# RWKV attention and a squared-ReLU feed-forward in one kernel: a new issue order of all steps, with two quarters of W2 loaded first

## The chip, the cores and the metric

One core of one Trainium2 chip. The metric is device time in microseconds for one launch; lower is better.

## The reference

Per batch and head a 48x48 state decays by `w` each step, takes in the outer product of k and v, and is read with r; `u` weighs the present step. The result, 3072 tokens of 384 numbers, goes through a feed-forward with a squared ReLU:

```python
batch, n_heads, seq, head_dim = (4, 8, 768, 48)      # r, k, v; w, u: n_heads x head_dim
for t in range(S):
    cur = np.einsum('bhd,bhe->bhde', u[None] * kt, vt)
    y[:, :, t] = np.einsum('bhd,bhde->bhe', rt, state + cur)
    state = w[None, :, :, None] * state + np.einsum('bhd,bhe->bhde', kt, vt)
...
n_tokens, d_model, d_ff = (3072, 384, 2048)
h = np.maximum(x @ w_in, 0.0)
return (h * h @ w_out).astype(np.float32)
```

## The kernel before

The tokens are cut into 24 tiles of 128 (tile i is chunk i // 4 of batch i % 4, so the state of a tile comes from tile i - 4). Every piece of work is a *step* with a short name, and one long string, `ORDER`, lists all steps. A step reads `name.arguments:engine/buffers`: `kh.4:G/5` is step kh of tile 4 on GpSimd with buffer 5. The engine letters are P (TensorE, PE in the profile), D (VectorE, DVE), A (ScalarE, ACT), G (GpSimd, POOL) and S (SyncE, SP, which only issues transfers). The string is walked once and each step is put on its engine's queue; an engine runs its queue strictly in the order of the string, and semaphores between engines see to it that data are there and buffers free. There is no other scheduler. `POOLS` says how many buffers each kind has (7 for loads of r, k and v, 2 PSUM banks for F1, 2 for F2, 4 for the rest of PE's work).

The steps of an attention tile, with the lines of the kernel before:

- `ld.r`, `ld.k`, `ld.v` (L320): load 128 tokens, 192 KB each, in rows of 192 bytes.
- `kh`, `rh` (L336, L339): k and r times powers of w, to `rk`. `T` and `Tc` (L363, L260) transpose `rk` on PE and copy it to `rkT`; `XB` (L369) does both as one DMA transpose issued by SP.
- `A` (L376) multiplies them, `Bm` (L384) masks the product. `P0`, `P1`, `du`, `dv` (L342, L346, L349, L354) make the part with u. `vb` (L260, L262) turns v to bf16.
- `Y` (L392, L394) is the tile's output, `xs` (L411) adds dv to it; `U` (L403), `ts` (L421), `S0` and `S` (L418, L424) carry the state on.
- `X` and `xTc` (L429, L260) transpose the output on PE and copy it to `xT`; `xX` (L436) does both as a DMA transpose issued by SP.

The feed-forward works on groups of tiles: tiles 0 and 1 alone (groups 0 and 1), then eleven groups of two. `F1.g.s` (L445) makes 512 numbers per row of the hidden layer of group g: s is a slice of 256 columns of `w_in` for a pair, and two such slices for a single tile. `re` (L453, L455) is the ReLU out of PSUM, which frees the F1 bank, and `sq` (L460, L462, L464) squares it. `F2.i.q` (L472) adds quarter q of the hidden layer to the output of tile i: four matmuls of 384 columns with `W2[q]`. After the four quarters `os` (L260, L262) copies the bank and `out` (L487) stores it.

The weights come in float32. `lW.0.s` (L324, by SP) loads slice s of `w_in` to one of four staging buffers and `cW.0.s` (L260, L262) casts it. `W.0.2` and `W.1.q` (L333, by POOL) are transfers that cast on the way: slice 2 of `w_in` and the four quarters of `w_out`. So W2 comes through POOL's DMA queue, and all else through SP's (or, for the stores marked A, ACT's). `w`, `u`, `wc`, `shw`, `shu`, `logw`, `Wk`, `Wt` and their like prepare the powers of w once. `Z.n.b` (L481) is n matmuls on the identity whose result nobody reads.

Early in the order stand the loads of tiles 0 to 3 and the slices of `w_in`, then the first F1 (`F1.1.0`), and only then `W.1.0`, `W.0.2`, `W.1.1`, `W.1.2`, `W.1.3`.

Of the kernel before, what the change touches and what calls it, by code (L numbers as in the profile page):

```python
# [20 lines left out]
ld.r.1:S/0 w:A ld.k.1:S/0 u:S Z.48.5:P tab:A ld.k.0:S/1 ld.k.2:S/2 shw:D ld.r.0:S/1 logw:A ld.r.2:S/2 Wt:A/0 P0.1:D/0  # L21
Wk:A/1 lW.0.6:S/0 kh.1:D/0 ld.v.1:S/0 rh.1:D shu:D ld.k.3:S/3 T.1:P/0 kh.0:D/1 Z.16.5:P P1.1:G Tc.1:A/0 kh.2:D/2
rh.0:D ld.v.3:S/1 WtS:A rh.2:D P0.2:G/1 A.1:P/1/2 WkS:A T.0:P/3 lW.0.1:S/1 Z.16.5:P P1.2:D ld.r.3:S/3 Tc.0:A/1
du.1:D/0 P0.0:D/2 cW.0.6:A ld.v.0:S/2 A.0:P/0/3 dv.1:G Bm.1.1:D/0 Z.6.5:P du.2:D/1 T.2:P/2 P1.0:G Bm.1.0:D/1
ld.v.2:S/3 Z.22.5:P Tc.2:A/2 Bm.0.0:D/2 Bm.0.1:D/3 lW.0.0:S/2 vb.1:A/0 lW.0.5:S/3 kh.3:D/3 Y.1:P/1 cW.0.1:A lW.0.7:S/0
A.2:P/0/2 xs.1:D/0 Z.4.5:P P0.3:G/3 vb.3:A/1 du.0:D/2 lW.0.4:S/1 X.1:P/3 Z.8.5:P rh.3:D wc:S xTc.1:A/0 Bm.2.0:D/4
vb.0:A/2 T.3:P/1 ld.k.4:S/4 dv.0:D Y.0:P/3 Z.13.5:P Tc.3:A/3 vb.2:G/3 Bm.2.1:D/5 P1.3:G xs.0:D/1 A.3:P/0/2 X.0:P/1
cW.0.0:A U.0:P/3 dv.2:G Bm.3.0:D/1 Z.6.7:P xTc.0:A/1 du.3:D/3 lW.0.3:S/2 F1.1.0:P/0 Bm.3.1:D/0 ld.r.4:S/4 F1.0.0:P/1
re.1.0:D/0 cW.0.7:G Y.2:P/0 Y.3:P/1 re.0.0:A/1 ld.k.5:S/5 xs.2:D/2 cW.0.5:A W.1.0:G dv.3:D F1.1.3:P/0 cW.0.4:A W.0.2:G
X.2:P/2 F1.0.3:P/1 re.1.3:D/2 ld.r.5:S/5 xTc.2:A/0 W.1.1:G U.2:P/0 xs.3:D/3 F1.0.2:P/0 re.0.3:A/3 sq.1.3:D2/0 WLcol:A  # L30
X.3:P/2 F1.1.2:P/1 re.0.2:D/4 xTc.3:A WLm:G U.3:P/1 F1.2.1:P/0 re.1.2:A/5 W.1.2:G sq.0.3:A0/1 F1.2.5:P/1 re.2.1:D/2
W.1.3:G sq.0.0:A0/2 U.1:P/2 S0.2:D re.2.5:A/3 F1.2.4:P/0 sq.0.2:D2/3 cW.0.3:A S0.0:D F1.2.7:P/1 re.2.4:D/1 sq.1.0:A0/4
# [36 lines left out]
S.11:D re.6.5:A/0 ts.13:D/0 F2.9.2:P os.8:A/2 out.7:S P0.18:D/0 sq.6.0:A0/5 Y.13:P/2 ts.12:D/1 ld.k.21:S/3
sq.6.6:A0/13 F2.9.3:P P1.18:G xs.13:D/3 sq.6.5:A0/15 ld.v.16:S/1 F2.10.0:P/1 Bm.14.1:D/2 dv.14:G X.13:P/0 du.15:D/0  # L70
F2.10.1:P ld.r.20:S/4 P0.16:G/4 re.6.7:D/2 xTc.13:A Y.14:P/1 vb.15:A/6 F1.7.5:P/0 kh.20:G/6 xs.14:D/4 ld.k.22:S/6
os.9:A/0 F1.7.6:P/1 S.12:D A.16:P/2/3 xX.14:S/0 re.7.6:A/1 P1.17:G A.17:P/0/1 F2.11.0:P/0 sq.6.7:A0/16 Bm.17.1:D/1
sq.6.4:A0/17 S.13:G F1.7.1:P/1 ld.v.20:S/6 Bm.16.1:D/0 re.7.5:A/4 F2.11.1:P ld.k.19:S/5 Bm.17.0:D/2 dv.15:G Y.15:P/1
re.7.1:D/3 ld.r.19:S/6 F1.7.0:P/0 xs.15:D/0 rh.20:G F1.7.3:P/1 re.7.0:A/0 ld.r.23:S/5 P1.16:D U.15:P/3 sq.7.1:A0/20
F2.10.2:P du.16:D/1 re.7.3:A/2 U.14:P/0 xX.15:S F1.7.2:P/0 P0.20:D/1 vb.16:A/3 dv.16:G Bm.16.0:D/3 sq.7.3:A0/18
F1.7.4:P/1 out.5:S re.7.2:A/5 rh.18:D F2.11.2:P vb.18:A/1 out.8:S sq.7.6:D2/21 re.7.4:A/3 F2.10.3:P sq.7.5:D2/19
ld.r.21:S/2 kh.19:D/5 vb.17:A/2 F1.7.7:P/0 ld.k.23:S/1 sq.7.4:A0/22 rh.19:D Y.16:P/1 kh.22:D/4 re.7.7:A/2 Y.17:P/2
XB.19:S/4 xs.16:D/2 sq.7.2:A0/23 F2.11.3:P kh.21:D/2 os.10:A/3 F1.8.2:P/1 du.17:D/2 sq.7.0:A0/26 XB.18:S/6 ts.14:D/1
F1.8.0:P/0 dv.17:G re.8.2:A/1 F2.12.0:P/1 os.11:A/2 re.8.0:D/4 vb.20:G/0 sq.8.2:A0/25 F1.8.3:P/1 xX.16:S/1 S.14:G
# [30 lines left out]
    A=["bA{0}0", "bA{0}1"],  # L110
    ld=["{0}{1}"],
# [7 lines left out]
def kernel(  # L119
# [417 lines left out]
```

## Time and profile before

| | |
|---|---|
| median of 3 runs | 176.94 us (176.59 to 178.07) |
| span of the profiled execution | 175.6 us |
| PE busy | 165.1 us (94%), 1813 matmuls |
| DVE / ACT / POOL busy | 140.6 / 109.4 / 69.2 us |
| read from and written to HBM | 20.46 and 4.72 MB |
| r, k, v loads | 72 of 192 KB, 3.8 to 4.1 us from issue to landing (medians) |
| W2 quarters (POOL's queue) | 4 of 384 KB as written, 10.2 us |
| transposes by DMA | 14 of rk (4.2 us), 10 of x (2.9 us) |
| granted PE clock | full in all slices |

The page gives no separate time for the profiled execution: its span is 175.6 us, and the runs' median is 1.3 us over it. A busy PE isn't PE at its peak, since matmuls are pipelined and their ends are modelled. What matters more is when PE stands still, and what it waits for there.

### The profile page before, as it was taken

To read this page: it belongs to the slowest core of one execution; us is meant where nothing else is said; L and a number is where in the kernel's file an instruction comes from. 1 tells how busy PE (TensorE), PEld (TensorE's weight loads), DVE (VectorE), ACT (ScalarE), POOL (GpSimd) and SP (SyncE) were. 2 spreads that over 40 slices of the span, in tenths; PEclk is the share of its full clock that TensorE was granted. 3 is DMA by queue.
4 is the path that set the end of the run, shared out by engine and by line. 5 is a ranking of instruction groups with operands and counts; after the bars stand their busy time and mean duration, and the time that the engine had idled before them with its cause. 6 is when DMAs were issued, how large, how long until landed. Compare 5 with 4: busy or idle time off the path is not lost.

```text
span 175.6 us, 4601 instructions
## 1 busy us (share of the span) xinstructions
PE 165.1 (94%) x1813; PEld 127.0 (72%) x1813; DVE 140.6 (80%) x278; ACT 109.4 (62%) x203; POOL 69.2 (39%) x84
## 2 busy tenths in 40 slices
PE   4888797899999999999999999999999999999991
PEld 4767695666778778777767787777778677787760
DVE  4699877499899998999989899899988667853620
ACT  2479498249399987886668669669478132164401
POOL 4073582035358394926282960600960302000000
PEclk9999999999999999999999999999999999999999
DMA  5999999989899999999999979989971422110041
GB/s 105 218 217 236 315 231 187 192 166 220 163 210 106 246 207 134 232 159 242 170 162 214 212 142 223 155 203 191 199 157 26 157 90 62 33 45 0 4 169 55
DMA packets 102277, 28.36 MB, mean 161 GB/s; under 512 B 94824, under 2 KB 102256, under 8 KB 102256
## 3 DMA queue, kind: packets, MB, share of 16 engines
q1 hardware_dynamic: 100360, 26.10, 75.4%
q0 software_dynamic: 1744, 1.77, 6.1%
q8 instruction: 14, 0.23, 0.6%
q10 hardware_dynamic: 152, 0.20, 0.3%
q14 instruction: 7, 0.06, 0.1%
HBM read 20.46 MB, written 4.72 MB: 143 GB/s over the span
## 4 chain that ended last, share of the span: by engine, by line
PE 80%; DMA 10%; SPq 4%; POOL 1%; issue 1%; ACT 0%; POOLq 0%
PE bank L472 36%; PE bank L445 33%; DMA wsa<-in_moe_w_in_dram 6%; DMA W<-in_moe_w_in_dram 5%; SPq L320 4%; PE bank L376 3%; PE bank L394 2%; PE bank L392 2%; PE bank L403 2%; PE bank L363 2%; PE bank L429 1%; POOL W L262 0%; SPq L324 0%; POOL W L333 0%; ACT os L260 0%
## 5 line engine op out<-in xcount | busy, mean ns | idle before, releaser
L445 PE MATMUL bank<-xT,W 128*128 128x256 bf16 (+1 forms) x624 | 74.4, 264 | 1.6 <-ACT W L260 0.9
L472 PE MATMUL bank<-W,hq 128*128 128x384 bf16 x384 | 73.6, 326 | 1.0 <-DMA W<-in_moe_w_out_dram 1.0
L453 ACT ACTIVATE hr<-bank 128x512 bf16<-128x512 f32 x71 | 42.0, 597 | 38.9 <-PE bank L445 36.3
L445 PEld LDWEIGHTS <-W 128*128 128x128 bf16 x624 | 55.3, 98 | 12.3 <-ACT W L260 1.2
L472 PEld LDWEIGHTS <-hq 128*128 128x128 bf16 x384 | 35.6, 98 | 19.0 <-issue 1.2
L460 ACT ACTIVATE hq<-hr 128x512 bf16<-128x512 bf16 x57 | 34.7, 629 | 2.5 <-DVE hr L455 2.4
L384 DVE TENSOR_TENSOR Bm<-bank,maskJT 128x512 bf16<-128x512 f32 x48 | 31.4, 683 | 3.0 <-PE bank L376 3.0
L346 POOL TENSOR_TENSOR P<-P,ub 128x384 f32<-128x384 f32 x14 | 15.2, 1086 | 35.5 <-DVE P L342 29.8
L455 DVE TENSOR_SCALAR hr<-bank 128x512 bf16<-128x512 f32 x25 | 17.1, 689 | 11.9 <-PE bank L445 8.3
L354 POOL TENSOR_TENSOR dv<-ldv,du 128x384 f32<-128x384 f32 x19 | 16.6, 886 | 23.7 <-DVE du L349 21.6
L464 DVE TENSOR_TENSOR hq<-hr 128x512 bf16<-128x512 bf16 x35 | 15.0, 457 | 1.7 <-ACT hr L453 1.7
L411 DVE TENSOR_TENSOR xs<-bank,dv 128x384 bf16<-128x384 f32 x24 | 13.2, 553 | 2.8 <-PE bank L394 2.2
L260 ACT COPY os<-bank 128x384 f32<-128x384 f32 x18 | 8.6, 477 | 8.1 <-PE bank L472 8.1
L481 PE MATMUL bank<-identity 128*128 128x128 bf16 x139 | 11.0, 242 | 2.3 <-POOL identity masks.py:199 2.3
L349 DVE TENSOR_REDUCE du<-P 128x8 f32<-128x384 f32 x24 | 12.9, 544 | 0.2 <-POOL P L346 0.2
L342 POOL TENSOR_TENSOR P<-ldr,ldk 128x384 f32<-128x384 f32 x11 | 11.3, 1024 | 2.4 <-DMA ldr<-in_r_dram 2.4
L260 ACT COPY rkT<-bank 128x1024 bf16<-128x1024 bf16 x10 | 10.1, 1015 | 2.8 <-PE bank L363 2.7
L481 PEld LDWEIGHTS <-identity 128*128 128x128 bf16 x139 | 9.7, 111 | 2.5 <-POOL identity masks.py:199 2.3
L424 POOL TENSOR_TENSOR S0W<-ts,WLm 128x384 bf16<-128x384 f32 x7 | 7.4, 1060 | 10.0 <-PE bank L472 6.7
L394 PE MATMUL bank<-vb,Bm 128*128 128x48 bf16 x192 | 10.8, 183 | 0.4 <-ACT vb L260 0.3
L394 PEld LDWEIGHTS <-Bm 128*128 128x128 bf16 x192 | 9.5, 96 | 1.4 <-issue 0.6
L260 ACT CAST vb<-ldv 128x384 bf16<-128x384 f32 x19 | 9.6, 512 | 0.0
(61 smaller groups left out, 163.8 us busy)
## 6 DMA issues: line engine op xcount, KB each, us to landing
ldr<-in_r_dram SPq DMA_DIRECT2D x24, 192.0 KB, 4.0
ldk<-in_k_dram SPq DMA_DIRECT2D x24, 192.0 KB, 4.1
ldv<-in_v_dram SPq DMA_DIRECT2D x24, 192.0 KB, 3.8
out_dram<-os SPq DMA_DIRECT2D x23, 192.0 KB, 2.1
wsa<-in_moe_w_in_dram SPq DMA_DIRECT2D x7, 384.0 KB, 4.8
W<-in_moe_w_out_dram POOLq DMA_DIRECT2D x4, 384.0 KB, 10.2
rkT<-rk SPq DMA_TRANSPOSE x14, 4.2
W<-in_moe_w_in_dram POOLq DMA_DIRECT2D x1, 192.0 KB, 8.1
```

Source lines behind the costliest of these rows:

```text
L260: e.copy(o, a)
L346: e.tensor_mul(t, t, ub)
L354: e.tensor_mul(dvb[slot[f"dv{i}"]], loaded("v", i), t)
L384: e.tensor_mul(Bmb[slot[f"Bm{i}{h}"]], heads(bank(f"bA{i}{h}"), 128), mask_b)
L394: e.matmul(y[:, hc, D * h : D * (h + 1)], m[h][:, hc, :], vb[:, 2 * hc + h, :], start=(c == 0), stop=True, skip_group_check=True,)
L445: e.matmul(hp[:, fi, :], W1[f // 2][:, c, 128 * (f % 2) : 128 * (f % 2 + 1)], xt[:, c, :], start=(c == 0), stop=(c == CCH - 1), skip_group ...
L453: e.activation(hr, hp, AF.Relu)
L455: e.tensor_scalar_max(hr, hp, 0.0)
L460: e.activation(hq, hr, AF.Square)
L464: e.tensor_mul(hq, hr, hr)
L472: e.matmul(bank(f"bO{i}", "bO")[:, 0:d_model], hqb[slot[f"hq{g},{f // m}"]][:, at : at + L], W2[q][:, f % 4, :], start=(f == 0), stop=(f = ...
L481: e.matmul(banks[b][:, 0:128], identity, identity, start=True, stop=True, skip_group_check=True)
```

## The change

`ORDER` is written anew from its first step to its last: 952 steps in place of 961, with the same buffers (`POOLS`) and the same groups. What differs beside the order:

- F2 takes a tile's quarters in any order. A list per tile notes which have been issued, so that the first starts the sum in PSUM and the last ends it.
- `W.1.2` and `W.1.3` are the first things that POOL issues after its setup, and `W.1.0` follows `P1.0`. The first F1 is `F1.1.3`, which uses slices 6 and 7, so these two are loaded first; the first F2 uses quarter 3. `lW.0.4` and `lW.0.5` now come behind the loads of tiles 4 and 5.
- 11 stores are issued by ACT (before: 1) and 13 by SP (before: 23).
- 16 x tiles are transposed by DMA (before: 10), 8 by PE (before: 14); of their copies 4 go to ACT and 4 to DVE (before: 14 to ACT). `XB` stays at 14.
- Work goes from DVE and ACT to POOL: kh 16 steps there (before 5), P0 18 (11), P1 18 (14), S 10 (7), rh 8 (6), vb 7 (3), cW 3 (1); dv goes the other way, 10 (19). ACT has 62 of the squares (before 57) and 69 of the ReLUs (71).
- The warm-up matmuls Z number 151 (before 139), 80 of them in front of the first T.
- `rh` may come before `kh` of the same tile, so it names the buffer too.

The order's beginning and end, and the code:

```diff
 ORDER = """
-ld.r.1:S/0 w:A ld.k.1:S/0 u:S Z.48.5:P tab:A ld.k.0:S/1 ld.k.2:S/2 shw:D ld.r.0:S/1 logw:A ld.r.2:S/2 Wt:A/0 P0.1:D/0
-Wk:A/1 lW.0.6:S/0 kh.1:D/0 ld.v.1:S/0 rh.1:D shu:D ld.k.3:S/3 T.1:P/0 kh.0:D/1 Z.16.5:P P1.1:G Tc.1:A/0 kh.2:D/2
-rh.0:D ld.v.3:S/1 WtS:A rh.2:D P0.2:G/1 A.1:P/1/2 WkS:A T.0:P/3 lW.0.1:S/1 Z.16.5:P P1.2:D ld.r.3:S/3 Tc.0:A/1
-du.1:D/0 P0.0:D/2 cW.0.6:A ld.v.0:S/2 A.0:P/0/3 dv.1:G Bm.1.1:D/0 Z.6.5:P du.2:D/1 T.2:P/2 P1.0:G Bm.1.0:D/1
-ld.v.2:S/3 Z.22.5:P Tc.2:A/2 Bm.0.0:D/2 Bm.0.1:D/3 lW.0.0:S/2 vb.1:A/0 lW.0.5:S/3 kh.3:D/3 Y.1:P/1 cW.0.1:A lW.0.7:S/0
-A.2:P/0/2 xs.1:D/0 Z.4.5:P P0.3:G/3 vb.3:A/1 du.0:D/2 lW.0.4:S/1 X.1:P/3 Z.8.5:P rh.3:D wc:S xTc.1:A/0 Bm.2.0:D/4
-vb.0:A/2 T.3:P/1 ld.k.4:S/4 dv.0:D Y.0:P/3 Z.13.5:P Tc.3:A/3 vb.2:G/3 Bm.2.1:D/5 P1.3:G xs.0:D/1 A.3:P/0/2 X.0:P/1
-cW.0.0:A U.0:P/3 dv.2:G Bm.3.0:D/1 Z.6.7:P xTc.0:A/1 du.3:D/3 lW.0.3:S/2 F1.1.0:P/0 Bm.3.1:D/0 ld.r.4:S/4 F1.0.0:P/1
-re.1.0:D/0 cW.0.7:G Y.2:P/0 Y.3:P/1 re.0.0:A/1 ld.k.5:S/5 xs.2:D/2 cW.0.5:A W.1.0:G dv.3:D F1.1.3:P/0 cW.0.4:A W.0.2:G
-X.2:P/2 F1.0.3:P/1 re.1.3:D/2 ld.r.5:S/5 xTc.2:A/0 W.1.1:G U.2:P/0 xs.3:D/3 F1.0.2:P/0 re.0.3:A/3 sq.1.3:D2/0 WLcol:A
-X.3:P/2 F1.1.2:P/1 re.0.2:D/4 xTc.3:A WLm:G U.3:P/1 F1.2.1:P/0 re.1.2:A/5 W.1.2:G sq.0.3:A0/1 F1.2.5:P/1 re.2.1:D/2
...
-re.12.7:A/5 F2.21.2:P re.12.4:A/3 sq.12.7:D1/24 F2.21.3:P F1.12.0:P/0 os.21:D/0 F2.20.0:P/1 re.12.0:A/2 F1.12.2:P/1
-F2.20.1:P re.12.2:D/5 F1.12.3:P/0 sq.12.0:D2/25 sq.12.1:D2/8 F2.20.2:P sq.12.6:D2/4 re.12.3:A/2 sq.12.2:D2/3
-F2.23.0:P/0 sq.12.4:D2/28 sq.12.3:A0/7 F2.20.3:P sq.12.5:A0/0 F2.23.1:P os.20:D/2 F2.23.2:P out.20:S F2.23.3:P
-out.19:S F2.22.0:P/1 out.21:S os.23:D/1 F2.22.1:P out.23:S F2.22.2:P F2.22.3:P os.22:A/2 out.22:A
+ld.k.1:S/0 ld.r.0:S/0 ld.r.1:S/1 u:S w:A ld.k.0:S/1 ld.k.2:S/2 wc:S ld.r.2:S/2 ld.k.3:S/3 ld.r.3:S/3 ld.v.1:S/0 shw:D
+tab:A P0.1:D/0 shu:D logw:A Wk:A/0 lW.0.7:S/0 W.1.2:G Wt:A/1 WkS:A ld.v.0:S/1 kh.1:D/0 rh.1:D lW.0.6:S/1 W.1.3:G WtS:A
+P1.1:G kh.0:D/1 Z.80.5:P T.1:P/0 rh.0:D Tc.1:A/0 Z.18.5:P A.1:P/1/2 WLcol:A T.0:P/3 rh.2:D/2 kh.2:D Bm.1.0:D/0 du.1:D/0
+Tc.0:A/1 T.2:P/0 P0.0:G/1 Tc.2:A/2 lW.0.0:S/2 lW.0.1:S/3 vb.1:A/0 P1.0:G Bm.1.1:D/1 W.1.0:G P0.2:G/2 Z.9.5:P A.0:P/1/3
+rh.3:D/3 kh.3:D ld.v.3:S/2 cW.0.7:A Z.16.5:P T.3:P/2 WLm:G vb.0:A/1 lW.0.3:S/0 ld.v.2:S/3 du.0:D/1 Y.1:P/0 Bm.0.1:D/2
+dv.1:G ld.k.5:S/4 P0.3:G/3 Bm.0.0:D/3 ld.r.5:S/4 Tc.3:A/3 xs.1:D/0 Z.20.5:P X.1:P/3 ld.k.4:S/5 dv.0:G ld.r.4:S/5
+ld.v.5:S/4 P1.3:D cW.0.6:A Y.0:P/1 Z.8.5:P A.3:P/0/2 lW.0.4:S/1 xs.0:D/1 X.0:P/1 xTc.1:D/0 F1.1.3:P/0 xTc.0:A/1
+Bm.3.1:D/4 W.0.2:G P1.2:G A.2:P/3/1 W.1.1:G re.1.3:A/0 F1.0.3:P/1 Bm.3.0:D/5 du.3:D/2 cW.0.0:G lW.0.5:S/2 dv.3:G
+re.0.3:D/1 Bm.2.1:D/0 U.1:P/2 U.0:P/0 cW.0.1:A ld.r.7:S/6 sq.1.3:A0/0 du.2:D/3 sq.0.3:A0/1 vb.3:A/2 Bm.2.0:D/1 S0.0:D
+F1.1.0:P/0 cW.0.3:G dv.2:D F1.0.0:P/1 F2.1.3:P/1 re.1.0:A/2 re.0.0:A/3 ld.v.4:S/5 Y.3:P/1 ld.k.7:S/6 F2.0.3:P/0 vb.2:A/3
+F1.1.1:P/0 U.3:P/3 Y.2:P/0 xs.3:D/2 ld.r.6:S/1 sq.1.0:D2/2 F1.0.1:P/1 S0.3:D ld.k.9:S/0 ld.k.6:S/1 U.2:P/1 F2.1.0:P
+ld.v.6:S/6 re.1.1:A/4 ld.r.8:S/0 X.3:P/3 kh.5:G/4 ld.v.8:S/0 xs.2:D/3 rh.5:G kh.4:G/5 P0.5:D/4 sq.1.1:A0/3 re.0.1:A/5
+ld.k.10:S/2 P0.4:G/0 F2.1.1:P sq.0.0:A0/4 ld.k.8:S/3 xTc.3:A/0 vb.5:G/4 X.2:P/0 S0.2:D xTc.2:A F2.0.0:P T.5:P/1 cW.0.4:G
+rh.4:D P0.7:G/1 Tc.5:A/4 S0.1:D F1.2.2:P/0 ld.k.13:S/4 rh.6:G/6 kh.7:G/0 sq.0.1:D2/5 ld.r.9:S/2 T.4:P/3 F1.2.7:P/1
+Tc.4:A/5 P1.5:D ld.r.13:S/3 U.5:P/0 P1.4:D ts.5:D/0 re.2.7:D/0 ld.v.7:S/1 F2.0.1:P P0.6:G/3 re.2.2:A/1 kh.6:G P1.6:G
+A.5:P/2/1 Bm.5.1:D/2 A.4:P/3/0 F1.2.4:P/0 cW.0.5:A P1.7:G ld.r.10:S/4 ld.v.13:S/2 Bm.5.0:D/3 F1.1.2:P/1 kh.8:G/1
...
+sq.11.7:D2/25 F2.20.2:P/1 F1.12.6:P/1 sq.11.1:A0/26 out.18:A sq.11.0:A0/0 re.11.3:A/4 sq.12.0:D2/24 sq.11.3:D2/10
+out.17:S re.12.6:D/0 F2.20.3:P F2.21.0:P F2.21.3:P F1.12.4:P/0 F1.12.3:P/1 re.12.4:A/1 re.12.3:D/5 F2.21.1:P
+sq.12.3:D2/29 F1.12.2:P/0 out.16:A re.12.2:A/3 sq.12.2:D2/1 F2.20.1:P F1.12.7:P/1 re.12.7:D/2 F2.20.0:P sq.12.6:D2/28
+F1.12.1:P/0 os.20:A/1 sq.12.7:A0/5 out.20:S F1.12.5:P/1 re.12.1:D/4 re.12.5:A/5 os.21:A/0 sq.12.1:D2/27 sq.12.5:D2/2
+F2.23.3:P/1 F2.23.1:P sq.12.4:D2/12 out.21:S F2.22.3:P/0 F2.23.0:P F2.22.1:P F2.23.2:P F2.22.2:P os.23:D/2 out.19:S
+F2.22.0:P os.22:A/1 out.23:S out.22:A
 """
...
-    lW=["ws{0}{1}"], kh=["rk{0}"], P0=["P{0}"], du=["dv{0}"], vb=["vb{0}"], T=["bT{0}"], Tc=["rkT{0}"], XB=["rkT{0}"],
+    lW=["ws{0}{1}"], kh=["rk{0}"], rh=["rk{0}"], P0=["P{0}"], du=["dv{0}"], vb=["vb{0}"], T=["bT{0}"], Tc=["rkT{0}"], XB=["rkT{0}"],
...
+    quarters = {}
...
         def F2(e, i, q):
             g, j = group_of[i]
             n = len(GROUP[g])
             m = 4 // n
+            done = quarters.setdefault(i, [])
+            done.append(q)
             for f in range(4 * q, 4 * q + 4):
                 at = L * n * (f % m) + L * j
                 e.matmul(
                     bank(f"bO{i}", "bO")[:, 0:d_model],
                     hqb[slot[f"hq{g},{f // m}"]][:, at : at + L],
                     W2[q][:, f % 4, :],
-                    start=(f == 0), stop=(f == FCH - 1), skip_group_check=True,
+                    start=(f == 4 * q and len(done) == 1), stop=(f == 4 * q + 3 and len(done) == 4),
+                    skip_group_check=True,
                 )
```

## The prediction, made before the changed kernel was run

> **What bounds the kernel now.** I read the slices first, then busy time by stretch, then PE's waits, then the DMA queues. Two rows of the slices, PE and the DMA engines:
>
> ```profile
> PE   4888797899999999999999999999999999999991
> ...
> DMA  5999999989899999999999979989971422110041
> ```
>
> A slice is 4.4 us. PE is full from the tenth slice to the last; the DMA engines are full from the second to the thirtieth (131 us). Two resources are nearly used up, so the question is where one feeds the other. Busy time by stretch (PE is the first number after the length):
>
> ```profile
> core 0: us, PE busy (x) PEld busy (x) DVE busy (x) ACT busy (x) POOL busy (x), PEclk, DMA share, GB/s
> 20.50:29.10 8.60, 8.55 (x130) 7.72 (x131) 6.32 (x13) 7.12 (x15) 5.29 (x8) 1.00 1.15 231
> 29.10:32.00 2.90, 1.18 (x11) 0.66 (x11) 1.09 (x3) 0.81 (x2) 0.00 (x0) 1.00 1.27 187
> 32.00:38.50 6.50, 6.50 (x63) 5.09 (x61) 4.97 (x11) 2.31 (x4) 0.48 (x1) 1.00 1.08 188
> 48.60:100.00 51.40, 51.40 (x593) 39.67 (x591) 48.55 (x91) 41.07 (x79) 31.70 (x33) 1.00 1.10 191
> 100.00:172.00 72.00, 71.96 (x679) 53.57 (x675) 54.00 (x104) 38.18 (x75) 17.51 (x19) 1.00 0.54 116
> ```
>
> From the first F1 (20.5 us, in the timeline) PE stands still for 1.8 us in all, at 29-32 us, and ends at 172.0. So 151.5 - 1.8 = 149.7 us of PE work follow the first F1, and the end is "first F1 + stalls + 149.7 + 3.6", the 3.6 being the last copy, store and close. Nothing that happens on DVE, ACT or POOL after 32 us sets the end. PE's stalls, and the transfers behind them:
>
> ```profile
> PE bank L472 <- DMA W<-in_moe_w_out_dram: 1.0, 1, 1.0
> PE bank L445 <- DMA W<-in_moe_w_in_dram: 0.7, 1, 0.7
> ```
>
> The start is paced by DMA. Queue lines of the DMA view for 28-36 us, then for 40-50 us (q0 is POOL's queue, q1 SP's):
>
> ```profile
> q0 software_dynamic: 1368, 1.28, 96.6%
> q1 hardware_dynamic: 1243, 0.24, 26.3%
> ...
> ldr<-in_r_dram SPq DMA_DIRECT2D x1, 192.0 KB, 6.8
> ...
> q1 hardware_dynamic: 10341, 1.96, 99.9%
> ```
>
> Alone, SP's queue moves 0.196 MB/us, one r/k/v load (0.197 MB) per 1.0 us. While POOL's W transfers run, the two queues take turns packet for packet (1368 against 1243), but a W packet is some 0.9 KB and a load packet 192 B: SP's queue falls to 0.03 MB/us, and a load waits for almost the whole W transfer. What five W transfers (W.1.0, W.0.2, W.1.1, W.1.2, W.1.3) cost SP's queue follows from two landings:
>
> ```profile
> 16.09 5.67 DMA wsa<-in_moe_w_in_dram
> ...
> 34.09 4.14 SPq L320 DMA_DIRECT2D ldr<-in_r_dram  x1
> ```
>
> The first (chain of waits) is lW.0.7: by 21.8 us 12 loads and 5 slices of w_in had landed, with no W running. The second (timeline) is ld.r.7; with the 6.8 above it landed at 40.9, as the 19th load, after all 7 slices and all W. 19.1 us for 7 loads (7.0), 2 slices at 1.3 (2.6; slices landed 1.1 to 1.5 apart) leaves 9.5 us for the five W: 2.1 per quarter of W2, 1.2 for W.0.2.
>
> **The change, part by part.** *F2 quarters in any order*: the same 4 matmuls of 163 ns, 0.65 us; only the accumulation flags move. Nothing, and nothing hides it. The entry in HELD is bookkeeping.
>
> *Six x tiles from PE to DMA* (8 left of 14). PE loses 6 x 0.17 us (L429, 3 matmuls at 56 ns) = 1.0 us, directly on the path. ACT loses ten copies of 478 ns, DVE gains four. SP gains six transposes of 1.2 us issue (median of L436), the DMA engines six times about 0.73 us (384 packets each). They lie in DMA's full stretch: 4.4 us, more than the 1.0 won, but hidden as long as loads lead. By summing SP's transfers against PE's steps, V loads reach PE 4 us or more ahead of their Y in both orders (least: v.19 before, v.18 after), and XB transposes at least 1 us ahead of A before, 2.7 after. So zero; if the cover goes, at most 4.4.
>
> *Ten stores more on ACT* (11 instead of 1). SP's issue of a store has a median of 530 ns, the one on ACT took 353: 3.5 to 5.3 us on an ACT that is 62% busy and loses 10 copies (4.8), 7 vb (3.6) and 2 casts (1.8) while it gains 5 squares (3.1). The new wait: in the built program a transfer waits for the one eight places before it, so a store on ACT can wait for SP. Behind it stand the next re and sq, and for re waits PE, which has two F1 banks. By the same sum the eighth transfer before has landed some 6 us or more before each of the eleven. Zero; once that lead is gone, every microsecond beyond one F2 (0.65) is PE's.
>
> *DVE to POOL*: kh on POOL 5 to 16, P0 11 to 18, P1 14 to 18, S 7 to 10, rh 6 to 8, vb 3 to 7, cW 1 to 3, dv 19 to 10, at 0.9 to 1.1 us each: POOL from 69 to some 95 us, DVE -8, ACT -10. POOL stays the least loaded of the four; hidden by the lead of the loads. Twelve more warm-up matmuls lie before the first F1, where PE waits anyway.
>
> *Two quarters of W2 first.* This decides. POOL now issues W.1.2 and W.1.3 at about 2.8 us, W.1.0 after P0.0 and P1.0 (about 12 us), W.0.2 and W.1.1 after dv.0 (21 to 24 us). Before, all five were issued from 22.6 us, behind everything that the first F1 needs. In front of SP's queue now: ld.v.2 is the 12th load, behind 5 slices, as in the 21.8 above. A W issued at 21 to 24 moves 2.6 us later (before: issue 22.6, first POOL packet 25.2), while v.3, lW.0.3 and v.2 are still to come, so all five W run ahead of v.2: 21.8 + 9.5 + 0.2 (wc, now early) - 0.5 (holes of the load queue at 4-13 us, DMA share 0.82 to 0.88 in the worst microseconds, that W fills) = 31.0. With the last two W behind v.2 it would be 27.7; with no filled hole and 0.5 lost in each of two more ramps, 32.5. I take 31.0: the issue times are nearer to it.
>
> Then: cast vb.2 (0.51) and Y.2 at 31.7. Ahead of Y.2 stands only 5.8 us of PE work from F1.1.3 (7 F1 or F2, Y.3, A.2, three U), which is issued at about 22 (lW.0.6 and its cast), so PE stalls 3 to 4 us. From Y.2 to the last matmul: 94 F2 at 0.651, 88 F1 at 0.655, 3 short F1 at 0.666, 20 A at 0.33, 20 Y at 0.36 and one at 0.33, 17 U and 6 X at 0.17, 6 T at 0.45 = 141.6. The same sum over the kernel before, from F1.3.0 at 48.6 us, gives 122.6 against 123.4 measured, so +0.7%: 142.5. End of PE 31.7 + 142.5 = 174.2, which is 2.2 later than 172.0.
>
> A second gate does not depend on the order inside the queue: F1.1.2 needs lW.0.5, now the last slice, behind 17 loads, 7 slices and all W: 21.8 + 5.0 + 2.6 + 9.5 + 0.2 - 0.5 = 38.6, cast 0.9, so its second half starts at 39.5; from the start of F1.1.2 to the end the same counting gives 133.8 x 1.007 = 134.7: end 39.2 + 134.7 = 173.9, 1.9 later. Two gates, 1.9 and 2.2; the later one counts.
>
> Total: -1.0 (X) and -1.8 (old stalls) and +0.5 (A.2 and U.0 moved behind the first F1), then the later start and the new stalls, +4.5: +2.2. The page gives the profiled execution a span of 175.6; the median of the runs, 176.94, lies 1.3 around it. 177.8 + 1.3 = **179.1 us**.
>
> [...]
>
> **The rivals.** *W2 rides free (faster).* If the first two quarters filled only what the load queue leaves idle, their 4.2 us would cost it nothing: v.2 at 26.8, lW.0.5 at 34.4, F1 at about 20, nothing to wait for, PE end 20 + 149.2 = 169.2, in all 174.1. It decides where v.2 lands before 28. For it: the DMA row begins with a 5. Against it: the 9s after it, and q1 at a quarter beside q0. *The start evens out (no change).* W.0.2 or W.1.1 slip behind v.2, and the load queue packs 1 us tighter: lW.0.5 at 37.5, end 172.8, in all 177.7. *The middle breaks too (slower still).* The six transposes, 4.4 us on a queue that is full to 131 us, eat the loads' lead, and x tiles reach F1 late: some 2 us more, 181.2. For it: x.6 and x.7 go to DMA just before F1.4, 3.4 us ahead by the sum, and a transpose takes up to 4.0 to land. Against it: the least lead of V is 4 us in both orders.
>
> **How the numbers follow.** Forecast (178.7 to 180.6) 0.42, no change 0.27, free ride 0.14, middle 0.17. A measurement of this kernel tells about 1% from nothing: faster 0.14, same 0.27, slower 0.59. The range takes in the no-change case and most of the middle one: 176.3 to 181.6.
>
> **What would show it.** Right: lW.0.6 lands after 20 us and ld.v.2 after 30; between 22 and 33 us PE stands still for 3 us or more, waiting for casts of W1 (L260, L262) or for Y.2's vb; q0 is busy from about 5 us and q1 sinks beside it; after 41 us PE has no gap. Wrong: v.2 before 28 us, or first F1 before 20.5 (free ride); ACT idle before a store, or PE waiting at L445 for a DMA of xT after 60 us (middle).

## The result, and the profile after

The changed kernel takes 192.06 us (median; 191.75 to 193.31) against 177.05 us for the kernel before on the same chip: 1.087 times the time, 95% interval 1.081 to 1.093. That is 15 us slower, far outside the predicted 176.3 to 181.6. The profiled execution has a span of 190.0 us, 14.4 more than before. Now and then a run takes 1 to 2% longer than others of the same kernel; the intervals here leave such runs out, but the traces of e1 and g4 below (199.8 and 187.76 us) are of such runs, so what is read from them is rough. Five rows of its slices (4.75 us each; PE, DVE and POOL busy, the granted PE clock, the DMA engines):

```profile
PE   5949998798799359999989999999999999999992
...
DVE  4439585899969996599999899889996998654540
...
POOL 7257571949699982485349695256665500000000
PEclk9985899999999966999999999999999999999999
DMA  6999999998996017949779799698797711511132
```

From the sixteenth slice on (71 us) PE is nearly as full as it was before. What is lost is lost ahead of that: in the start and the smaller gaps behind it, and in a hole at 60 to 69 us (the 3) with a reduced clock behind it (6 and 6). In the hole the DMA engines stand still (0 and 1), while DVE is at 9 and POOL at 9 and 8. By stretch (PE first after the length, then weight loads, DVE, ACT, POOL, clock, DMA share):

```profile
23.42:40.00 16.58, 14.93 (x197) 11.20 (x198) 12.82 (x23) 11.13 (x19) 10.03 (x11) 1.00 1.05 217
40.00:50.00 10.00, 8.06 (x104) 6.33 (x101) 9.59 (x15) 7.97 (x16) 7.59 (x7) 1.00 0.93 183
50.00:60.00 10.00, 10.00 (x94) 7.30 (x95) 8.13 (x13) 5.59 (x11) 9.32 (x10) 1.00 1.05 208
60.00:68.70 8.70, 3.90 (x55) 3.20 (x53) 8.70 (x12) 5.02 (x9) 8.62 (x8) 0.95 0.01 2
68.70:75.18 6.48, 6.48 (x34) 3.23 (x35) 4.79 (x10) 0.00 (x0) 2.30 (x4) 0.54 0.53 101
100.00:186.40 86.40, 86.25 (x836) 64.33 (x833) 69.16 (x123) 44.93 (x85) 32.81 (x34) 1.00 0.63 132
```

The first F1 starts at 23.42 us (20.50 before): +2.9. From there PE idles 1.65 us to 40 us, 1.94 to 50, 4.80 at 60 to 68.7, 0.5 at 75 to 100 and 0.15 after that, 9.0 in all against 1.8 before: +7.2. After the hole it runs for 6.48 us at a granted clock of 0.54: +3.0. With the 1.0 us of transposes less and 0.5 us moved behind the first F1 this makes 12.6 of the 14.4; I could not place the rest. PE's waits in the middle all end on DVE:

```profile
PE bank L474 <- DVE hq L464: 1.9, 1, 1.9
PE bank L429 <- DVE xs L411: 1.8, 2, 1.0
PE bank L392 <- DVE Bm L384: 1.3, 1, 1.3
PE bank L392 <- DVE ts L421: 1.2, 1, 1.2
```

DVE has 267 instructions instead of 278, but 148.4 us of work instead of 140.6. The groups of its squares, of its `rh` and of its `Bm`, first before, then after (busy us, mean ns):

```profile
L464 DVE TENSOR_TENSOR hq<-hr 128x512 bf16<-128x512 bf16 x35 | 15.0, 457 | 1.7 <-ACT hr L453 1.7
L339 DVE TENSOR_TENSOR rk<-ldr,Wt 128x384 bf16<-128x384 f32 x14 | 7.9, 576 | 0.0
L384 DVE TENSOR_TENSOR Bm<-bank,maskJT 128x512 bf16<-128x512 f32 x48 | 31.4, 683 | 3.0 <-PE bank L376 3.0
```

```profile
L464 DVE TENSOR_TENSOR hq<-hr 128x512 bf16<-128x512 bf16 x31 | 19.1, 620 | 2.5 <-ACT hr L453 2.3
L339 DVE TENSOR_TENSOR rk<-ldr,Wt 128x384 bf16<-128x384 f32 x12 | 9.6, 804 | 0.6 <-DMA ldr<-in_r_dram 0.6
L384 DVE TENSOR_TENSOR Bm<-bank,maskJT 128x512 bf16<-128x512 f32 x48 | 31.2, 678 | 1.9 <-PE bank L376 1.7
```

The same instructions have become longer, but not `Bm`, which reads PSUM: 683 and 678 ns. What has become longer has all its operands in SBUF. The timeline of DVE and POOL in the hole shows why (start, length):

```profile
57.56 2.37 POOL L342 TENSOR_TENSOR P<-ldr,ldk 128x384 f32<-128x384 f32 x2
57.73 1.35 DVE L339 TENSOR_TENSOR rk<-ldr,Wt 128x384 bf16<-128x384 f32 x1
59.01 1.21 DVE L464 TENSOR_TENSOR hq<-hr 128x512 bf16<-128x512 bf16 x1
59.90 1.18 POOL L346 TENSOR_TENSOR P<-P,ub 128x384 f32<-128x384 f32 x1
60.14 0.68 DVE L384 TENSOR_TENSOR Bm<-bank,maskJT 128x512 bf16<-128x512 f32 x1
60.74 0.62 DVE L464 TENSOR_TENSOR hq<-hr 128x512 bf16<-128x512 bf16 x1
61.04 1.18 POOL L424 TENSOR_TENSOR S0W<-ts,WLm 128x384 bf16<-128x384 f32 x1
61.28 1.35 DVE L354 TENSOR_TENSOR dv<-ldv,du 128x384 f32<-128x384 f32 x1
```

The square that starts at 59.01 ends at 60.22, 0.29 us behind the end of POOL's P0 (59.93); the next one ends at 61.36, 0.28 behind P1 (61.08); dv at 62.63, 0.41 behind S (62.22). Each ends a fixed time behind the POOL instruction that was running, as if it had waited for it, and POOL's next one then takes longer too (S 1.18 us; 0.99 to 1.00 where no such DVE instruction runs beside it). `Bm` runs through beside P1. In the whole trace 34 of 79 DVE multiplications within SBUF are more than 60 ns longer than undisturbed, and all 34 end either 0.28 us (squares) or 0.41 to 0.42 us (float32) behind the end of a POOL instruction. With five casts of vb, which have one operand, that is 39 stretched instructions and 19.8 us lost; before there are 12 (one a cast), and 5.2 us. The same count is used for every run below.

Two rows that answer to the queue lines of before: POOL's queue beside SP's at 5 to 10 us, and what SP waits for ahead of the hole.

```profile
q0 software_dynamic: 481, 0.71, 83.3%
q1 hardware_dynamic: 1090, 0.21, 25.1%
```

```profile
SPq L436 <- DVE xs L411: 15.1, 3, 12.4
```

W2 pushes the loads aside at 5 to 10 us too, with 0.71 MB against 0.21. And SP, which issues in order, stands 12.4 us at `xX.6` because DVE has not made xs.6; the loads behind it are not issued, hence the idle DMA engines. That is a consequence of DVE's delay, not its cause: e4 below takes `xX.6` away, the DMA engines then work half of the time from 60 to 70 us (0.52), and the hole stays.

### The profile page after: what moved, and what is told of

Its sections match the earlier page's. It is cut to its first block, busy times and chain, and to the rows that moved or that the text cites. A ratio compares the mean times of both kernels' runs of the same rounds, so it can differ in the third digit from the quotient of the medians.

```text
span 190.0 us, 4564 instructions
## 1 busy us (share of the span) xinstructions
PE 171.4 (90%) x1807; PEld 129.7 (68%) x1807; DVE 148.4 (78%) x267; ACT 102.9 (54%) x184; POOL 97.2 (51%) x108
## 4 chain that ended last, share of the span: by engine, by line
PE 58%; DVE 18%; DMA 10%; SPq 4%; POOL 3%; issue 2%; ACT 2%; DVEq 0%; ACTq 0%
PE bank L474 28%; PE bank L445 22%; DMA ldk<-in_k_dram 5%; DMA wsa<-in_moe_w_in_dram 4%; SPq L320 3%; DVE hq L464 3%; DVE Bm L384 3%; PE bank L376 3%; DVE dv L354 3%; DVE rk L339 2%; DMA ldr<-in_r_dram 2%; PE bank L394 1%; DVE hr L455 1%; DVE xs L411 1%; PE bank L392 1%
## 5 line engine op out<-in xcount | busy, mean ns | idle before, releaser
L460 ACT ACTIVATE hq<-hr 128x512 bf16<-128x512 bf16 x62 | 37.1, 625 | 3.6 <-DVE hr L455 1.6
L342 POOL TENSOR_TENSOR P<-ldr,ldk 128x384 f32<-128x384 f32 x18 | 20.6, 1149 | 10.3 <-DMA ldk<-in_k_dram 9.5
L346 POOL TENSOR_TENSOR P<-P,ub 128x384 f32<-128x384 f32 x18 | 20.0, 1113 | 9.3 <-DVE P L342 6.7
L464 DVE TENSOR_TENSOR hq<-hr 128x512 bf16<-128x512 bf16 x31 | 19.1, 620 | 2.5 <-ACT hr L453 2.3
L336 POOL TENSOR_TENSOR rk<-ldk,Wkhat 128x384 bf16<-128x384 f32 x16 | 17.2, 1080 | 6.1 <-DMA ldk<-in_k_dram 5.5
L411 DVE TENSOR_TENSOR xs<-bank,dv 128x384 bf16<-128x384 f32 x24 | 13.2, 548 | 6.3 <-PE bank L394 5.2
L258 ACT COPY rkT<-bank 128x1024 bf16<-128x1024 bf16 x10 | 10.1, 1010 | 14.2 <-PE bank L363 14.1
L424 POOL TENSOR_TENSOR S0W<-ts,WLm 128x384 bf16<-128x384 f32 x10 | 10.7, 1074 | 9.7 <-DVE ts L421 7.2
L484 PE MATMUL bank<-identity 128*128 128x128 bf16 x151 | 12.7, 258 | 2.3 <-POOL identity masks.py:199 2.3
L484 PEld LDWEIGHTS <-identity 128*128 128x128 bf16 x151 | 11.7, 120 | 2.5 <-POOL identity masks.py:199 2.3
L354 POOL TENSOR_TENSOR dv<-ldv,du 128x384 f32<-128x384 f32 x10 | 8.7, 878 | 6.7 <-DMA ldv<-in_v_dram 3.8
L392 PE MATMUL bank<-S0W,rkT 128*128 128x96 bf16 x80 | 9.8, 204 | 2.5 <-DVE Bm L384 1.3
```

What stands on the lines that cost most here:

```text
L258: e.copy(o, a)
L336: e.tensor_mul(rk[slot[f"rk{i}"]][:, 1, :, 0:D], loaded("k", i), early("WkP") if i < EARLY else Wkhat)
L342: e.tensor_mul(P0b[slot[f"P{i}"]], loaded("r", i), loaded("k", i))
L346: e.tensor_mul(t, t, ub)
L460: e.activation(hq, hr, AF.Square)
L464: e.tensor_mul(hq, hr, hr)
```

## The experiments

Theory at first ("POOL"): the work moved to POOL stretches DVE, and DVE becomes the path. Rivals: START (W2 ahead of the loads), SP (transposes hold up the loads), ACT (stores).

**Undoing one part at a time.** Four kernels, each the changed one with one part as before. (The kernel before took 176.72 us beside them.)

```diff
 e1, 89 steps like these
-P0.4:G/0 ... dv.5:D ... vb.5:G/4
+P0.4:D/0 ... dv.5:G ... vb.5:A/4
 e2
-W.1.2:G ... W.1.3:G ... W.1.0:G ... W.0.2:G ... W.1.1:G
+W.0.2:G W.1.3:G ... W.1.1:G W.1.0:G W.1.2:G
 e3, ten like this
-out.3:A
+out.3:S
 e4, six like this
-xX.6:S/2
+X.6:P/2 xTc.6:A/2
```

> The changed kernel with one part undone: kh, rh, P0, P1, S, dv, vb and the casts of W1 run on the engines that they had before (89 steps change engine; POOL loses 44 of them on balance, POOL's busy time goes back to some 70 us); order, W2 quarters, transposes and stores stay as changed. Theory POOL (POOL's extra work stretches the DVE instructions whose operands are all in SBUF, DVE becomes the path at 41 to 69 us, and PE's gaps cost clock): sq on DVE back from 620 to about 460 ns and rh from 804 to about 580, PE busy over 9.5 of 10 at 60 to 70 us, time 178 to 181. Theory START (the two W2 quarters ahead of the loads make most of the loss): 189 to 192, the start unchanged. Theory SP (the transposes x.6 and x.7 in SP's queue hold up the loads behind them): 188 to 192, DMA still idle for some 10 us after 60. Theory ACT (stores on ACT): 190 to 193.

> The changed kernel with one part undone: POOL issues the three quarters W.1.3, W.1.0 and W.1.2 behind W.0.2 and W.1.1 (in all W.0.2, W.1.3, W.1.1, W.1.0, W.1.2, from about 20 us), nothing else moves. Theory POOL: the start gets 2 to 4 us better, the gap at 60 to 70 us stays: 187 to 191. Theory START: 177 to 180. Theory SP and theory ACT: 189 to 192.

> The changed kernel with one part undone: ten of ACT's eleven stores are issued by SP at the same places of the order (all but out.22, as before). Theory POOL and theory START: 191 to 194, no change or up to 1 us slower, since SP gets ten issues of 0.53 us back. Theory ACT: 178 to 182. Theory SP: 191 to 195.

> The changed kernel with one part undone: the six further x tiles (6, 7, 9, 10, 13, 19) are transposed by PE again at the same places of the order, each followed by a copy on ACT; SP has six transposes fewer. Theory POOL: SP is no longer held by x.6, but DVE is as late as before, and PE now waits for xs.6 itself; PE gains 1.0 us of work: 187 to 192, DVE still full and its sq still above 580 ns at 60 to 70 us. Theory SP: loads flow on through 60 to 70 us (DMA share over 0.8), 179 to 183. Theory START and theory ACT: 192 to 194.

Measured: e1 196.95 us (ratio to the kernel before 1.107 to 1.122), e2 192.59 (1.086 to 1.100), e3 194.36 (1.089 to 1.107), e4 196.3 (1.107 to 1.120). None comes near 180. e1 and e4 are slower still than the changed kernel, e2 and e3 cannot be told from it, and every theory misses its number for its own part. e2, e3 and e4 keep the hole at 60 to 70 us (PE busy 5.35, 4.92 and 5.37 of 10), in e4 without `xX.6` in SP's queue. In e1 PE loses 0.8 to 1.5 us in each 10 us from 60 to 100, and DVE works more, not less (150.7 us; 29 instructions are still stretched, 14.2 us). A likely reason is in the order: ahead of F1.3.2, where PE has some 30 us of F1, F2 and attention behind it, the changed order has about 36 us of DVE steps (undisturbed durations, counted over the order), the order before about 39 at the same amount of PE work, and e1 about 45. The new order asks for later tiles' preparation sooner and relies on POOL for it, so engines can't be given back without the order; this was not tested by itself. Undoing does not separate the causes here; doing one part alone, and taking the conflict away without touching the work, do.

**The conflict by itself.** "LOCK" is the theory from the timeline above; "LOAD" says that the order asks too much of DVE too early, conflict or not. f1 and f2 are the kernel before plus 28 useless POOL instructions; only their kind differs.

```diff
 f1 (28 steps dm.n:G from F2.0.0 to F2.12.0)
+        def dm(e, n):
+            e.tensor_mul(dum[:, 0 : H * D], wb..., ub...)
 f2
+            e.memset(dum.bitcast(BF16), 0.0)
```

> The kernel before, plus 28 more multiplications on POOL, spread evenly over the order from F2.0.0 to F2.12.0: each multiplies two constants in SBUF (wb and ub, 128x384 fp32) into a scratch buffer that nobody reads. POOL's busy time goes from 69 to some 97 us, as in the changed kernel; DVE, ACT, PE and the transfers have the same work as before. In the changed kernel's trace 39 DVE instructions with two operands in SBUF are stretched (19.8 us lost in all; 12 and 5.2 us before), and each ends 0.28 us (sq) or 0.42 us (the fp32 ones) behind the end of a POOL instruction. Theory LOCK (such a DVE instruction waits for the end of the POOL instruction that is running): over 30 stretched, 10 to 16 us lost, and with DVE at 92 to 98% from 48 to 100 us the time is 181 to 188. Theory LOAD (the changed order asks DVE and POOL for too much work of later tiles too early, and would be slow without any contention): POOL has idle time for the dummies, 177 to 178.5.

> The kernel before, plus 28 memsets on POOL at the same places of the order, about 1 us each (1024 bf16 in each partition; 768 took 0.74 us in the setup), into the same scratch buffer: POOL is as busy as with the multiplications but these instructions read nothing. [...] Theory WIDE (any busy POOL slows DVE): as the multiplications.

f1 takes 189.48 us, 1.069 times the kernel before (1.064 to 1.075); f2 178.35, 1.007 (1.003 to 1.010). The groups of the added instructions and of DVE's squares, first f1, then f2:

```profile
L485 POOL TENSOR_TENSOR dum<-wb,ub 128x384 f32<-128x384 f32 x28 | 31.4, 1122 | 0.7
L462 DVE TENSOR_TENSOR hq<-hr 128x512 bf16<-128x512 bf16 x35 | 18.3, 550 | 1.7 <-ACT hr L451 1.7
```

```profile
L485 POOL MEMSET dum<- 128x1024 bf16 x28 | 26.7, 952 | 0.5
L462 DVE TENSOR_TENSOR hq<-hr 128x512 bf16<-128x512 bf16 x35 | 15.0, 456 | 1.7 <-ACT hr L451 1.7
```

Multiplications that touch nobody's data cost 12 us; memsets at the same places 1. In f1, 35 DVE instructions are stretched and 20.1 us lost, in f2 17 and 7.6. In f2 27 of DVE's multiplications within SBUF ran beside memsets alone, and none was longer than 0.56 us: undisturbed. So useless POOL multiplications in the old order can cost 12 us, and LOCK is shown as a cause of that size, and the form of it for DVE's multiplications: POOL's multiplications, which read SBUF, stretch them; its memsets, which read nothing, do not. (f1 is slower than the 181 to 188 expected of LOCK; f2 is 11 us below the multiplications' time, where WIDE had it.) DVE's casts of vb, which have one operand, are another matter: in g1 below, where POOL runs memsets, four of five were stretched, and all four end 0.21 us behind the end of a memset. One of them takes 0.67 us instead of 0.35:

```profile
60.51 0.74 POOL L276 MEMSET P<- 128x768 bf16 x1
60.79 0.67 DVE L258 CAST vb<-ldv 128x384 bf16<-128x384 f32 x1
```

**Less POOL, less DVE.** f3 leaves out 18 P1 on POOL, f4 moves 13 squares to ACT; both are otherwise the changed kernel.

```diff
 f3
-P1.4:G ... (18 steps; these tiles' r*k is not multiplied by u)
 f4
-sq.1.0:D2/2 ... (13 steps)
+sq.1.0:A0/2
```

> The changed kernel with the 18 P1 that POOL has left out (for these tiles r*k is not multiplied by u), about 20 us of POOL's 97; DVE has the same instructions, and du no longer waits for P1. Theory LOCK: stretched DVE instructions fall from 39 to some 20 to 25, the loss from 19.8 to 8 to 12 us, the gap of PE at 60 to 70 us shrinks from 4.8 to under 2.5 us and the half clock after it goes: 180 to 186. Theory LOAD: DVE's own instructions are what is late; 187 to 191.

> The changed kernel with the 13 squares of groups 0 to 5 that DVE has (0.62 us each on average, 8 us with the stretch) on ACT instead (0.60 us each; ACT is busy 5.0 to 8.0 of each 10 us from 30 to 70 us). Theory LOCK and theory LOAD agree that DVE is the path at 41 to 69 us: the gap at 60 to 70 us shrinks from 4.8 us to 1 to 3 and the half clock behind it may go: 182 to 187. Theory START (what is lost is lost by 40 us, and DVE only follows): 190 to 193.

f3: 189.58 us (1.063 to 1.078), so some 2.5 us better where I expected 6 to 12; the time lies in LOAD's range, not in LOCK's. But the edit did not do what it was made for: POOL lost 20 us of work, and 33 DVE instructions are still stretched (18.0 us), so f3 doesn't decide between the two. Presumably what is left on POOL moves up and meets DVE elsewhere. In f3 POOL's busy time is no measure of the conflict. f4: 186.89 (1.048 to 1.065), 5 us better, as both theories have it: DVE is the path. PE is busy 9.08 of 10 at 60 to 70 us, and the clock there stays full (1.00).

**The changed kernel without the conflict, and each part alone.** In g1 POOL's 80 multiplications from tile 4 on become stand-ins that read one element in each partition and write the rest.

```diff
 g1
+    def mul(e, i, o, a, b):
+        if e is not nc.gpsimd or i < EARLY:
+            e.tensor_mul(o, a, b)
+        else:
+            e.tensor_mul(o[:, 0:1, 0:1], a[:, 0:1, 0:1], b[:, 0:1, 0:1])
+            z = o.bitcast(BF16) if o.dtype == FP32 else o
+            e.memset(z, 0.01)
+            e.memset(dum.bitcast(BF16)[:, 0 : 896 - z.free_size()], 0.01)
 g2, the order before
-P1.1:G ... P1.0:G ... W.1.0:G ... W.1.2:G ... W.1.3:G
+W.1.2:G W.1.3:G P1.1:G ... P1.0:G W.1.0:G
 g3, the order before, 89 steps like these
-P0.4:D/4 ... dv.5:G
+P0.4:G/4 ... dv.5:D
 g4, the order before, six like this
-X.6:P/3 ... xTc.6:A/2
+xX.6:S/2
```

> The changed kernel, with POOL's 80 multiplications from tile 4 on (kh, rh, P0, P1, S, dv) replaced by stand-ins of the same length: one multiplication of a single element in each partition, which waits for the same operands, then memsets over the output and a scratch buffer (896 bf16 in all). What these tiles compute is left out; order, waits, engines and transfers stay as changed. Theory LOCK: the stretched DVE instructions fall from 39 to under 15, the gap of PE at 60 to 70 us and the half clock after it go, the start stays as it is: 179 to 183. Theory LOAD (the changed order asks too much too early of DVE, with or without the lock): 186 to 191, with DVE still full and PE idle at 60 to 70 us. If the start costs what the prediction said, and nothing else, 179.

> The kernel before, with W.1.2 and W.1.3 as POOL's first steps and W.1.0 behind P1.0, as in the changed kernel; W.0.2 and W.1.1 and all else stay. By the prediction's reasoning (bytes of W move ahead of loads, packet for packet) the loads that the first F1 and Y.2 wait for land later: 177.5 to 180. If W fills holes only: 175.5 to 177.

> The kernel before, with kh, rh, P0, P1, S, dv, vb and the casts of W1 on the engines that the changed kernel gives them (89 steps change engine; POOL from 69 to some 95 us, DVE loses 8 us of work). Theory LOCK: this alone makes most of the loss; 30 to 45 DVE instructions stretched, 12 to 20 us lost against 8 us of work won: 182 to 190. Theory LOAD: 176 to 179.

> The kernel before, with the x tiles 6, 7, 9, 10, 13 and 19 transposed by DMA at the places of the order where PE transposed them; six copies less on ACT. The prediction's step (1.0 us of PE won, the transfers hidden by the loads' lead): 175.5 to 176.5. Its rival of the middle (transposes take the DMA engines' time while they are full, loads come late): 178 to 181.

Beside 178.03 us for the kernel before: g1 183.9 (1.030 to 1.047), g2 182.05 (1.020 to 1.030), g3 185.81 (1.039 to 1.050), g4 184.63 (1.033 to 1.044).

g1: 5 DVE instructions stretched, 1.4 us; the hole is gone.

```profile
60.00:68.70 8.70, 8.55 (x93) 6.13 (x91) 8.09 (x17) 5.61 (x11) 8.29 (x22) 1.00 0.58 120
```

POOL is as busy as ever (8.29 of 8.70), DVE does 17 instructions instead of 12 in the stretch, PE runs. The time is 0.9 us above LOCK's range and 2.1 below LOAD's. So some 8 of the 15 us are the conflict, and LOAD falls as an explanation of the hole. g3 comes to the same size from the other side: the engine letters alone, in the old order, cost 7.8 us. DVE loses 8 us of work and gains 13.3 us of waiting (35 stretched, 18.5 us), and its busy time goes from 140.6 to 145.6. This is the price of the whole step, not of the conflict alone: of PE's waits behind the first F1 4.4 us end on DVE, but 3.6 on casts that POOL has now:

```profile
PE bank L389 <- POOL vb L257: 2.6, 1, 2.6
PE bank L440 <- POOL W L257: 1.0, 1, 1.0
```

g2: W2 first costs 4.0 us alone, more than either expectation. Its first F1, with the wait ahead of it:

```profile
26.30 2.74 PE L440 MATMUL bank<-xT,W 128*128 128x128 bf16 x24 [2.28 <-ACT W L255]
```

In the kernel before these 24 matmuls started at 20.50 and took 1.51 us. In the trace k of tile 2 lands at 11.2 us instead of 7.0, and the last slice that the first F1 needs at 25.35 instead of 19.54; its cast ends just before 26.30. PE stands 2.5 us waiting for `rk`, the granted clock is 0.66 at 10 to 20 us, and 0.52 during the first F1, hence the 2.74 us.

g4: six transposes by DMA, put where PE did them, cost 6.6 us instead of winning 1.0, more than either expectation. F1 waits for them:

```profile
PE bank L440 <- DMA xT<-xs: 7.9, 4, 3.0
```

PE waits for the landing of single transposes, which take some 0.65 us by PE and ACT (0.17 and 0.48) and 2.3 to 4.8 us from issue to landing by DMA. In the changed order PE never waits for one, and without them (e4) it is slower.

**What is left, and whether any W may go ahead.** h1 is g1 with W2 late as in e2. h2 is the kernel before with ten stores on ACT. h3 and h4 move one and two W transfers of the kernel before into 1.5 us in which POOL stands idle ahead of a cast.

```diff
 h2, ten like this
-out.3:S
+out.3:A
 h3
-cW.0.7:G ... W.1.0:G ... W.0.2:G
+W.1.0:G cW.0.7:G ... W.0.2:G
 h4
+W.1.0:G W.0.2:G cW.0.7:G
```

> The kernel of g1 (the changed kernel with POOL's multiplications from tile 4 on replaced by stand-ins that read one element and write the rest; their results are left out), and POOL issues W.1.3, W.1.0 and W.1.2 behind W.0.2 and W.1.1, as in e2. If the remaining 6 us of g1 over the kernel before are the start (W2 ahead of the loads, 4 us when done alone in g2): 178 to 181. If they lie in the rest of the order (casts and rk that PE waits for at 30 to 40 us, the transpose at 70 to 80): 183 to 185.

> The kernel before, with ten stores more on ACT (out.3, 0, 5, 13, 11, 15, 14, 9, 16, 18) at their places of the order. The prediction's step (nothing): 176.5 to 178.5. If a store that waits for the eighth transfer before it holds ACT's queue up: 179 to 183, with an idle time of ACT ahead of a store in the profile.

> The kernel before, with one step moved: POOL issues W.1.0 ahead of the cast cW.0.7, where it stands idle for 1.5 us (waiting for lW.0.7 until 21.8 us); W.1.0 and the W behind it go out 2.3 and 0.9 us sooner. In the kernel before PE waits 1.0 us for W.1.0 and 0.7 us for W.0.2 at 29 to 32 us. If nothing else becomes late: 1.0 to 1.7 us faster, 175 to 176.5. By the lesson of g2 (W ahead of loads makes the loads late): no gain or slower, up to 179.

> The kernel before, with two steps moved: POOL issues W.1.0 and W.0.2 ahead of the cast cW.0.7; the cast goes some 0.2 us later. If nothing else becomes late: 1.5 to 1.8 us faster, 175 to 176. By the lesson of g2: lW.0.3 and the loads of tiles 4 and 5 land later, no gain or slower, up to 180.

Beside 176.58 us: h1 182.23 (1.023 to 1.035), h2 177.35 (0.998 to 1.006), h3 175.84 (0.991 to 0.998), h4 175.66 (0.992 to 0.997).

h1 lies between the two expectations: by the ratios late W2 wins some 1.7 us, not 4 (the intervals of g1 and h1 overlap, so it may be nothing), and the changed order's first F2 then wait for their quarters (1.9 us) and its F1 for a cast of `w_in` (2.1). So of g1's 6 us the start is the larger part by PE's account (first F1 at 25.3 instead of 20.5 us), but moving the transfers alone did not remove it; how the rest splits stays open. h2: stores on ACT cost nothing that can be measured. h3 and h4 are half a per cent faster than the kernel before, as expected if nothing that matters becomes late: PE waits neither for W.1.0 nor for W.0.2, and at 20 to 40 us it is busy

```profile
20.00:30.00 10.00, 9.43 (x143) 8.59 (x144) 7.43 (x15) 8.17 (x17) 5.04 (x8) 1.00 1.20 236
30.00:40.00 10.00, 9.95 (x93) 7.42 (x91) 8.49 (x18) 6.02 (x12) 1.98 (x2) 1.00 0.95 173
```

in h3, against 8.55 and 9.18 before. In h3 W.1.0 was issued 2.9 us sooner (19.7 instead of 22.6 us). A slice of `w_in` then landed at 28.5 instead of 25.0 us and a load of r at 34.5 instead of 25.8, but PE waited for neither. In g2, with two quarters issued 23 us sooner, what came late was what the first F1 needs.

## Why the prediction was wrong

**The step that failed** is "DVE to POOL", put at nothing: "POOL stays the least loaded of the four; hidden by the lead of the loads." The cover named was the wrong one. The loads' lead may hide that POOL needs nearly twice the time for a step (P0 takes 0.99 to 1.01 us there and 0.55 on DVE, both undisturbed); it doesn't hide that POOL's steps stop DVE's (39 instructions, 19.8 us). "DVE -8" measured +7.8: 140.6 - 8 of work + 14.6 more of waiting is 147.2, and the profile has 148.4. The size was 7.8 us alone (g3, with POOL's late casts) and about 8 in the change (g1, the conflict). With it fell the premise that nothing on DVE after 32 us sets the end, which held in the kernel before. The rows of before had the sign of it: squares with a mean of 457 ns and single ones of 1.0 and 1.2 us, and DVE at 48.55 of 51.4 us from 48.6 to 100, in a window that the prediction showed and read only for PE.

**W2 first** had the right effect on the loads, and the wrong place for the stall. That the turns of 28 to 36 us (1368 packets against 1243) hold at 5 to 10 us too was the author's estimate; in the change q0 moved 481 packets there against q1's 1090. q1 sank to 0.21 MB beside q0's 0.71, lW.0.5 landed at 39.2 us (38.6 predicted) and ld.v.2 at 29.2 (31.0). But the five W did not all run ahead of v.2: W.1.1 landed at 32.2 us. And PE did not stand still for Y.2, which began at 29.8, right behind the cast vb.2. Of the 3 us or more that PE was to wait at 22 to 33 us for casts of W1 or for vb it stood still for 0.9, with one wait of 0.4, for a quarter of W2. That its idle time from the first F1 to 50 us adds up to 3.6 us, near the 3 to 4 predicted, is luck: it waited for the quarter (0.4), for S0 from DVE (0.5), for vb from POOL (0.4) and, at 47 to 50 us, for xs from DVE (1.0 and 0.8).

Mis-sized was the first F1, "about 22", at 23.42 in the change. lW.0.6 landed at 22.3 us and its cast ended at 23.37. By the prediction's own prices the landing comes out right: with two loads and three slices fewer than at its 21.8 us, and three quarters of W2 ahead, 21.8 - 2.0 - 3.9 + 6.3 = 22.2; what the 22 left out is the cast, 0.9 us, behind it. PE's own prelude, which waited 1.1 and 1.9 us for `rk` and ran at a clock of 0.51 from 13.2 to 20.1 us, ended at the same time, so it might have held the first F1 as long; that was not tried. F1.1.2 then came at 41.2 instead of 39.2 us. Alone, in the old order, the step cost 4.0 us (g2); the prediction's own terms for the change gave 4.5 - 1.8 = 2.7. The free-ride rival falls: v.2 landed after 28 us and the first F1 came after 20.5.

**Six x tiles.** "Hidden" held in the change (no wait of F1 for a transpose); the 1.0 us won was not measured by itself. Its fallback, "if the cover goes, at most 4.4", was the wrong quantity: it counted the DMA engines' time, while in g4, at 6.6 us, PE waits for landings.

**Ten stores**: zero held in the old order (h2). **F2 in any order** and the two steps moved behind the first F1 were not tried alone.

**The rival of the middle** had the right place and sign and the wrong cause: PE waits at DVE, not for xT. "After 41 us PE has no gap" was the sign that went wrong, beside the stall at 22 to 33 us and v.2 after 30.

## What to carry to other kernels

In this kernel, where DVE is nearly full, a multiplication within SBUF that is moved to POOL gave nothing: it takes 0.55 us off DVE, and in f1 each POOL multiplication put 0.53 us back (14.9 us over 28) by stopping another. In the changed kernel 13 squares given to ACT instead won 5 us (f4). POOL's memsets left DVE's multiplications alone (27 beside one in f2, none over 0.56 us), but not its casts (four of five in g1, up to 0.67 us instead of 0.35). And an edit that is costed at nothing needs its cover checked against every engine that the moved instruction can stop, not only against the data that it waits for.

## What the runs showed of the hardware

- A DVE multiplication with both operands in SBUF doesn't slow down evenly beside a POOL multiplication, its end follows POOL's: in the six traces counted in this way (before, changed, f1, f2, g1, g3) all 127 stretched ones end 0.28 or 0.41 to 0.42 us behind the end of a POOL instruction. POOL is lengthened in turn: in the change P0 takes 0.99 to 1.01 us with no such DVE instruction beside it and up to 1.3 with one (mean 1.15; 1.02 before). DVE instructions that read PSUM (Bm 683 and 678 ns) and the one-operand reduce (544 and 538 ns) are untouched.
- A memset on POOL stops no such multiplication: 27 beside one in f2, at 0.41 to 0.56 us. It does stop a DVE cast from float32 to bf16 within SBUF: four of five in g1, at 0.45 to 0.67 us instead of 0.35, each ending 0.21 us behind a memset.
- A hole in PE's work can be paid twice. With 4.8 us of idle time at 60 to 68.7 us, in pieces of at most 1.9 us, the granted clock was 0.54 for the next 6.5 us; at 13 to 20 us, with two gaps of 1.1 and 1.9 us at 10.9 to 14.7, it was 0.52. But the 0.9 us of the hole at 60 to 70 us in f4 cost no clock, nor did the 1.8 us at 29 to 32 us in the kernel before, nor a single gap of 2.6 us at 113 us in g3 (clock 1.00 from 105 to 130 us). No run here shows where the limit lies.
